# Strassen products with two-term weight sums, partial sums kept as PSUM seeds, and row sums shared with GpSimd

## The chip, the cores and the metric

The kernel runs on one core of a Trainium2 chip. The metric is the device time of one execution in microseconds (us); I give the median of the timed runs. Profiles are of one execution each, and a profile's span is a little shorter than the timed figure (276.0 against 278.06 us in the profiled execution of the kernel before). In the profile, PE is TensorE's matmuls, PEld its weight loads, DVE is VectorE, ACT is ScalarE, POOL is GpSimd, and SP issues DMAs.

## The reference

```python
x = A_x                                   # 1 x 2048 tokens x 512, bf16
for _ in range(2):
    x = x + attn(layernorm(x), wqkv, wo)  # linear attention, 32 heads of 16:
                                          #   phi(q) (phi(k)^T v) / (phi(q) . sum phi(k)),  phi(t) = t+1 or exp(t)
    x = x + relu(layernorm(x) @ w1) @ w2  # w1: 512 x 1376, w2: 1376 x 512
```

## The kernel before

The kernel builds a graph of about 1,400 operations. A fixed table, `ORDER`, lists them; each engine gets its own operations in the order of the table, runs them strictly in that order, and waits on semaphores for operations of other engines. A letter after an index chooses the engine of a flexible operation (`a` ACT, `d` DVE, and in the changed kernel `p` GpSimd). A second table, `BANKS`, gives each PSUM tile one of the eight banks. Two operations in different engines' lists have no order but what their data and their banks demand.

The second FFN product uses Strassen's seven products instead of eight, over pairs of 128-token tiles. It needs sums of hidden rows ("row sums", 128 x 1,280 elements in bf16) and sums of weight blocks, here up to four terms:

```python
T1, T2, T3, T4 = B12, w2s[:, 0, :, :], w2s[:, 1, :, :], w2s[:, 2, :, :]
tt(T3, B22, B12, ALU.add, ...)
tt(T1, B12, B11, ALU.subtract, ...)
tt(T2, B22, T1, ALU.add, ...)
tt(T4, B21, T2, ALU.subtract, ...)
...
def row_sums(t):
    def tt(n, a, b, rd):
        ap, key, own = sum_slot()
        g.add(DVE, lambda e: e.tensor_tensor(ap, a, b, ALU.subtract), ...)   # always on DVE
    tt(1, A21, A22, lo + hi)
    tt(2, A11, out[1][0], ...)
    tt(3, A21, A11, lo)
    tt(4, A12, out[2][0], ...)
```

Four times per pair, an intermediate product is scaled and added to the residual in SBUF:

```python
def part(i, bank, cols, name):
    g.add(DVE, lambda e: e.scalar_tensor_tensor(xres[:, i, cols], psv[:, bank, R], rstdf[:, i:i + 1],
                                                xres[:, i, cols], ALU.mult, ALU.add), ...)
prod("fy", raw(KH, l2), T4, ..., cb, L, True, l2)
prod("f1", raw(0, l1), B11, w, cb, R, False);           part(i1, cb, L, "r11")
prod("f5", summed(1), T1, ..., ca, R, True);            part(i2, ca, R, "r22")
prod("f6", summed(2), T2, ..., cb, R, False);           part(i1, cb, R, "r12")
...                                                     # f2, f3, f7
part(i2, cb, L, "r21")
```

Two groups of small DVE operations will play a part. One is the attention's reciprocal of the denominators, whose result TensorE waits for; the other is the variance of a chunk of 512 tokens:

```python
g.add(DVE, lambda e: e.scalar_tensor_tensor(rsp[:, s, :], rhi[:, s, :], rneg[:, 0:1], lden[:, s, :], ...))   # "rsp"
mm_group(...)                                            # denominators broadcast to 4 banks: needs rsp
for j in range(4):
    g.add(DVE, lambda e, j=j: e.tensor_tensor(unit_ap(us[j]), unit_ap(us[j]), psv[:, GB[j], :], ALU.mult))   # frees the bank
...
g.add(DVE, lambda e: e.scalar_tensor_tensor(nm2f[:, sl], nmf[:, sl], -1.0, nmf[:, sl], ...))                 # 128 x 4
g.add(DVE, lambda e: e.scalar_tensor_tensor(varf[:, sl], s2f[:, sl], INV_D, nm2f[:, sl], ...))               # 128 x 4
```

Of the kernel before, what the change touches and what calls it, by code (L numbers as in the profile page):

```python
# [14 lines left out]
C_MM512 = 216.0  # L15
# [25 lines left out]
C_POOL_TT = 1250.0  # L41
C_POOL_CP = 700.0
# [27 lines left out]
class _Graph:  # L70
# [52 lines left out]
    def add_flex(self, alts, reads=(), writes=(), name=""):  # L123
# [7 lines left out]
17 0 14 12 15 18 13 1 16 19 2 20 22 3 24 4 21 23 25 5 6 26 27 7 28 8 33 29 47 30 31 32a 34 48 40 49 35 71 50 36 41 42  # L131
51 37 43 52 73 44 38 72 53d 45 74 39a 87 56 46a 76 54 89 88 58 81 78 60 77 98 59 55 57 61 83 62 75 63 82 93 117 100
113 86 99 64 65d 66a 108 79 80 68a 90 69 103 84 67a 85 119 92 95 70 115 94 135 114 91 110 118 116 120 105 141 121 154
122 104 158 130 109 156 136 132 123 125d 131 124d 142 126d 138 128 133 157 137 155 148 139 127d 143 134 129 230 149
160 147 159 140 161 153 162 96 163 97 144 219 171 101 106 150 102 164 177 172 166d 165d 173 145 189 169 168d 167a 146
151 183 191 152 170 190 107 176 192 178 222 193 184 220 182 9 111 112 179 10 221 201 185 11 174 223 180 181 231 203
186 175 213 202 187 204 188 214 205 215 195 216 217 207 196 197 232 209 194 198 208 199 210 200 211 233 206 234 261
212 262 218 263 224 228 225 264 229 265 244 235a 237d 238a 236d 249 246 226 245 266 251 259 267 250 269 239 268 276
260 240 241 270 315 313 277 252 311 247 317 316a 314d 254 278 318d 312a 271 279 248 256 253 334 255 242 257 273 243
344 335 272 258 329 338 336 345 337a 319 330 339 320 346 331 347d 332a 301 340 321 349 341 291 342d 333 322 302 296  # L140
323 350 292 274 293 324 275 306 298 280 294 303 327 286 297 299 304 307 328 281 287 295 358 288 300 326 282 362 359d
308 283 305 364 325 348 284 355 363a 285 365a 309 388 310 343 289 227 376 356a 389 357 374 377a 290 392 390 437 375d
378 438 403 351 391d 379 352 353 372 354 439 404 380 360 373d 381 398 361a 440 382 370 399 368 441 371a 402 400 405
383 369a 366 386 401a 387 393 367a 385 406a 477 384 478 394 409 442 397 475 462 395 473 396a 452 444 407 457 408 453
447 443 456 454 474 493 455a 480 448 494 449 451 446 496 450a 463 423 464 466 445 467 417 424a 465d 476 421 418a 410
479 419 422a 411 412 481 413 414 458 420a 427 459 461 460d 497 415a 468 433 495 428a 469 425 470 434a 471 472 416 431
426d 572 429 432a 435 430a 482 436a 484 483 488 500 489 521 501 522 498 570 485 499 490 526 502 486 504 550 505 487
491 531 503 527 492 506 536 532 551a 507 547 525 509 556 508 510 571 548a 558 511 557a 512 573 513 549 530 560 523 528
537 529a 552 514 515d 516a 518d 562 561a 517d 519 559a 538 566 524d 563a 539d 553a 533 520 574 534d 567a 543 575 535
554 541 576 540 577 555a 544 542 579 578 564 580 545 546 581 565a 582 585 583 590 586 584 593 587 591 594 588 568 592  # L150
589 597 569d 595 714 618 596 715 629 620 619 716 601 630 598 621 631 622 623 602 599 635 625 717 600 643 626 624 632
633 603 666 645 604 644 606 663 605 607 667d 670 664a 627 608 609 628 665 636 671a 668 638 610 646 637 647 648 669d
634 653 649 650 611 672 612d 613a 614d 678 673a 615d 616 654 639 718 679d 655 719 640 617 651 674 641 720 676 675a 652
656 680 677a 657 682 681a 684 683a 721 685a 723 722 737 724 734 738 792 735 741 736 793 742 794 739 729 740 725 730
743 745 795 726 731 746 799 727 747 642 800 728 732 796 744 748 803 733 750 686 751 749 797 687 812 798 688 752 801
753 754 689 815 802 813 816 755 807 814 756a 819 808 758a 757d 817 759d 760 809 820 818 810 823 761 690 804 811 824
691 658 805 821 806 693 659 825 692 826 695 694 699 696 828 822 697 700 829 827 698 660 762 830 702 831 661 832 701
707 703 662 764 704 706 709 833 705 708 776 763 834a 835d 713 710 778 711 838 769 765 836a 712 768 837a 771 766 775
839 779 770 767 783 777 772 846 785 780 773 784 782 786 774 848 847 840 849 787 791 842 781 841 852 843 873 850 854
788 853 858 874 875 844 845 789 860 859 851 855 856 790 888 857 889 861 862 890 866 876 867 877 863 868 891 892 895  # L160
864 896 865 897 898 878 869a 872d 870a 871d 905 880 899 879 893 881 906 882 907 900 894 883 903 910 901 885 884 902
949 945 912 904 915 911 950d 946a 951 947 886 952a 920 948d 917 887 978 921 908 918 909 922 973 979 916 923 963 980
974 981a 968 975 964 976a 965 967 953 969 984 940 954 966d 970 977 930 971d 919 983 955 913 925 924 942 956 941 935
914 957 931 932 1012 1166 958 926 960 927 992 962 1013 1010 961 993a 937 959 1002 1011a 933 928 1014 938 1008 934
1003a 929 1015 994 1009a 1016 936 1037 943 995a 944 972 939 1032 1038 982 985 1071 1033 1017 1072 998 1019 986 1073
1034 1039 987 1006 1035d 988 1040a 1018 1004 999a 1074 1043 1021 1007a 1000 1020 1005a 1075 996 1001d 1076 997d 989
1078 1027 990a 1077 991 1022 1028 1086 1029 1031 1023 1030a 1024 1091 1025d 1026 1079 1042 1081 1041 1109 1096 1036
1087 1111 1092 1090 1107 1112 1125 1082 1114 1097 1085 1126 1093 1113 1094a 1128 1088 1098 1108 1048 1100 1115 1051
1099a 1127 1083 1095 1089d 1116 1102 1110 1084a 1130 1118 1049a 1131 1101 1052a 1117 1119 1129 1080 1135 1050 1121
1120 1132 1136 1122 1133 1167 1137 1123 1150 1134 1138 1155 1124 1145 1151 1139 1140 1152 1156 1153a 1053 1146 1157  # L170
1147 1149 1055 1158d 1141 1148a 1063 1142 1144 1143d 1161 1061 1168 1159 1154 1180 1169 1160 1065 1056a 1044 1162
1064a 1163 1045 1103 1059 1164 1104 1054a 1165 1105 1046 1181a 1067 1062a 1106 1057 1066a 1060a 1176 1047 1069 1068a
1177 1058a 1182 1178 1070a 1184 1183a 1179 1197 1185a 1170 1267 1198a 1199 1171a 1265 1191 1200a 1201 1172 1266 1192a
1214 1202a 1186 1193 1195 1203 1268 1196a 1173 1194 1215a 1187 1208 1174a 1189 1204 1209a 1218 1175 1190a 1231 1188
1205 1210 1219a 1216 1223 1232d 1225 1224a 1217d 1212 1235 1213a 1226d 1220 1236a 1227 1206 1233 1207a 1221 1242 1250
1211 1243a 1222 1248 1234d 1251a 1269 1244 1237 1228 1254 1249a 1245 1238 1270 1229 1239 1271 1252 1230a 1246 1253a
1274 1247a 1255 1259 1272 1260a 1275 1240 1256 1273 1279 1241a 1261 1263 1280 1283 1264a 1262 1257 1281 1284 1258a
1282 1276 1298 1302 1285 1303 1299 1277 1304 1286 1278 1288 1287 1307 1300 1290 1289 1305 1301 1293 1308 1316 1294
1331 1317 1291 1306 1318 1309 1332 1295 1321 1292 1312 1322 1310 1296 1319 1311 1297 1335 1333 1336 1334 1326 1349
1337 1320 1338 1327 1350 1339 1323 1351 1313 1328 1324 1329 1340 1325 1314 1360 1341 1315 1354 1345 1330 1355 1352  # L180
1346 1356 1353 1361 1347 1342 1348 1362 1343 1357 1367 1358 1344 1363 1359 1366 1364 1368 1365
"""
BANKS = ("0145324562706310713073037377010377101337703107013101701070073333700656655033141302741603645322705013"
         "6431645710222077055722557250202702550722705057572520720507270507252572220575725077545320570423052463"
         "720156456671340275034631527643015276410235")


def _replay(ops, tile_ops, vbank, partial, seeded, order_s, banks_s):
# [15 lines left out]
    for pos, w in enumerate(table):  # L204
        o = ops[int(w.rstrip("ad"))]
        if o.alts:
            eng = {"a": ACT, "d": DVE}[w[-1]]
            o.eng, o.emit, o.dur = [x for x in o.alts if x[0] == eng][0]
# [24 lines left out]
    return order, max(o.t_done for o in ops)  # L233


def build_kernel(nc, A_x, A_wqkv, A_wo, B_w1, B_w2, out, n_layers_pairs=2, Q_LATE=3, O_PE_CHUNKS=3, PHI_PATH=3,
                 KV_LAG=2, INTERLEAVE=True, WARM=10, SPLIT_CHUNKS=1, TAIL_SPLIT=True,
                 PHI_K=3, PHI_QE=3, PHI_QL=3, ZH_FIRST=True, P2_TIGHT=False,
                 FIRST_PE_CHUNKS=1, TGK=2, TGF=2, FT_PE=0, WP_GB=True, WO_LAG=1, DEN_PRE=1, LATE_A=1, ZP=(0, 3), WK_ACT=False, ACT_STATS=(), REM_TOK=True, RSTD_ACT=(0, 1, 2, 3), FILL=(0,), NFILL=2, HEAD_DEP=0, ST_ACT=True, H_STR=[0, 1, 2, 3, 4], NSUM=6):
# [977 lines left out]
```

## Time and profile before

The median of three runs is 278.93 us (278.34 to 279.35); with a fourth run, as in the result below, it is 278.75. The lines below are from the profile page of the kernel before: the span, the busy times by engine with their share of the span, the busy tenths of PE and POOL in 40 slices of the span, the granted TensorE clock in tenths, and the chain of waits followed back from the last instruction.

```profile
span 276.0 us, 4814 instructions
...
PE 270.5 (98%) x1794; PEld 153.1 (55%) x1794; DVE 237.2 (86%) x600; ACT 178.0 (65%) x372; POOL 34.4 (12%) x43
...
PE   7999999999999999999999999999999999999995
...
POOL 3111000001002021032003464000000005000000
PEclk9999999999999999999999999999999999999999
...
PE 94%; DVE 2%; DMA 2%; ACT 0%; issue 0%; SPq 0%; DVEq 0%
```

TensorE is busy 98% of the time and every slice but the first and the last is at 9 tenths or more. The chain of waits stays on TensorE for 94% of the span. TensorE's own list of waits (line, what released it, us in total, times, longest) says the same:

```profile
PE ps L407 <- DVE wrm L400: 1.2, 1, 1.2
PE ps L486 <- DVE xn L967: 0.4, 1, 0.4
PE ps L523 <- DMA Tb<-xn: 0.3, 1, 0.3
PE ps L523 <- ACT Tb L493: 0.3, 1, 0.3
```

That is 2.2 us in the whole program. DVE is busy 86%, but nothing waits long for it.

One interaction is visible. GpSimd has few large operations before, the adds of 512 columns at L580. This is the timeline of the kernel before around one of them (start in us, duration, engine, line, operation):

```profile
...
158.31 0.43 DVE L509 TENSOR_TENSOR big<-big,emscr 128x512 bf16<-128x512 bf16 x1
...
158.82 1.16 POOL L580 TENSOR_TENSOR lden<-lden,big 128x512 f32<-128x512 f32 x1 [1.09 <-DVE big L509]
...
158.97 1.28 DVE L509 TENSOR_TENSOR big<-big,emscr 128x512 bf16<-128x512 bf16 x1
```

The DVE add takes 0.43 us when it runs alone and 1.28 us when it starts just after a GpSimd add: it ends 0.27 us after that one. I call the excess over an instruction's clear duration "held" time. Summed over the trace before, DVE is held for 8.5 us, all of it in the attention stages and none of it where TensorE waits.

### The profile page before, as it was taken

To read this page: it belongs to the slowest core of one execution; us is meant where nothing else is said; L and a number is where in the kernel's file an instruction comes from. 1 tells how busy PE (TensorE), PEld (TensorE's weight loads), DVE (VectorE), ACT (ScalarE), POOL (GpSimd) and SP (SyncE) were. 2 spreads that over 40 slices of the span, in tenths; PEclk is the share of its full clock that TensorE was granted. 3 is DMA by queue.
4 is the path that set the end of the run, shared out by engine and by line. 5 is a ranking of instruction groups with operands and counts; after the bars stand their busy time and mean duration, and the time that the engine had idled before them with its cause. 6 is when DMAs were issued, how large, how long until landed. Compare 5 with 4: busy or idle time off the path is not lost.

```text
span 276.0 us, 4814 instructions
## 1 busy us (share of the span) xinstructions
PE 270.5 (98%) x1794; PEld 153.1 (55%) x1794; DVE 237.2 (86%) x600; ACT 178.0 (65%) x372; POOL 34.4 (12%) x43
## 2 busy tenths in 40 slices
PE   7999999999999999999999999999999999999995
PEld 2444544344465657655877444443447745568883
DVE  5999669999996795998689777799999997978996
ACT  4998838996776195486254987689947279762000
POOL 3111000001002021032003464000000005000000
PEclk9999999999999999999999999999999999999999
DMA  6946950120142018003005030003022450300014
GB/s 207 381 99 112 292 161 0 37 41 20 38 78 57 0 21 153 2 20 76 2 0 59 20 76 0 2 1 76 4 57 40 95 148 8 38 0 2 0 78 152
DMA packets 41974, 18.32 MB, mean 66 GB/s; under 512 B 36352, under 2 KB 40544, under 8 KB 41952
## 3 DMA queue, kind: packets, MB, share of 16 engines
q1 hardware_dynamic: 41808, 17.96, 27.7%
q8 instruction: 14, 0.23, 0.3%
q10 hardware_dynamic: 144, 0.07, 0.1%
q14 instruction: 8, 0.07, 0.1%
HBM read 7.01 MB, written 2.10 MB: 33 GB/s over the span
## 4 chain that ended last, share of the span: by engine, by line
PE 94%; DVE 2%; DMA 2%; ACT 0%; issue 0%; SPq 0%; DVEq 0%
PE ps L523 93%; DMA xin<-in_A_x_dram 1%; DMA Tb<-xn 1%; DVE xres L536 1%; DVE xn L563 1%; PE ps L486 0%; DVE xn L543 0%; DVE bst L430 0%; ACT Tb L493 0%; DVE nmf L539 0%; SPq L371 0%; DVEq L1155 0%; DVE xn L967 0%; DVE emscr L507 0%; DVE big L509 0%
## 5 line engine op out<-in xcount | busy, mean ns | idle before, releaser
L523 PE MATMUL ps<-Tb,w 128*128 128x512 bf16 x260 | 61.1, 379 | 0.3 <-DMA Tb<-xn 0.3
L530 ACT ACTIVATE sqscr<-xres 128x512 bf16<-128x512 f32 x48 | 30.0, 626 | 24.7 <-DVE xres L567 19.1
L505 ACT ACTIVATE escr<-ps 128x512 bf16<-128x512 f32 x64 | 38.3, 615 | 7.5 <-PE ps L523 6.4
L523 PEld LDWEIGHTS ps<-Tb,w 128*128 128x128 bf16 x260 | 24.9, 98 | 28.4 <-DMA Tb<-xn 0.6
L503 ACT ACTIVATE big<-ps 128x512 bf16<-128x512 f32 x64 | 37.7, 615 | 3.8 <-PE ps L523 3.6
L893 DVE SCALAR_TENSOR_TENSOR xres<-ps,rstdf,xres 128x256 f32<-128x256 f32 x64 | 30.0, 480 | 9.0 <-PE ps L523 8.4
L724 ACT ACTIVATE big<-ps 128x512 bf16<-128x512 f32 x50 | 28.5, 598 | 9.4 <-PE ps L523 9.4
L523 PE MATMUL ps<-w,big 128*128 128x256 bf16 (+1 forms) x224 | 33.9, 273 | 0.0
L523 PE MATMUL ps<-Tb,wqkv 128*128 128x512 bf16 x138 | 33.2, 379 | 0.0
L509 DVE TENSOR_TENSOR big<-big,emscr 128x512 bf16<-128x512 bf16 x64 | 29.8, 479 | 2.1 <-ACT big L503 0.8
L523 PE MATMUL ps<-wqkv,Tb 128*128 128x512 bf16 x128 | 30.8, 379 | 0.3 <-ACT Tb L493 0.3
L523 PE MATMUL ps<-big,xn 128*128 128x512 bf16 x128 | 30.9, 379 | 0.0
L523 PE MATMUL ps<-Wp,big 128*128 128x512 bf16 x128 | 30.1, 379 | 0.0
L556 POOL TENSOR_TENSOR rstdf<-varf,nhalf 128x4 f32<-128x4 f32 x8 | 9.1, 1146 | 122.5 <-DVE varf L554 122.5
L523 PEld LDWEIGHTS ps<-w,big 128*128 128x128 bf16 (+1 forms) x224 | 21.8, 98 | 4.6 <-DVE xres L893 0.3
L523 PE MATMUL ps<-w,xin 128*128 128x256 bf16 x160 | 22.6, 272 | 0.0
L507 DVE TENSOR_SCALAR emscr<-escr 128x512 bf16<-128x512 bf16 x64 | 19.4, 317 | 3.1 <-ACT escr L505 2.9
L523 PEld LDWEIGHTS ps<-Tb,wqkv 128*128 128x128 bf16 x138 | 13.2, 98 | 15.5 <-issue 0.5
L523 PE MATMUL ps<-w2s,xin 128*128 128x256 bf16 x160 | 21.7, 273 | 0.0
L681 DVE TENSOR_TENSOR big<-big,ps 128x512 bf16<-128x512 bf16 x32 | 20.7, 681 | 0.4 <-PE ps L523 0.4
L523 PEld LDWEIGHTS ps<-wqkv,Tb 128*128 128x128 bf16 x128 | 12.1, 98 | 15.1 <-ACT Tb L493 1.0
L523 PEld LDWEIGHTS ps<-Wp,big 128*128 128x128 bf16 x128 | 12.1, 98 | 14.3 <-issue 0.5
(126 smaller groups left out, 379.6 us busy)
## 6 DMA issues: line engine op xcount, KB each, us to landing
wqkv<-in_A_wqkv_dram SPq DMA_DIRECT2D x3, 512.0 KB, 7.4
xin<-in_A_x_dram SPq DMA_DIRECT2D x3, 512.0 KB, 8.2
out_dram<-xn SPq DMA_DIRECT2D x3, 512.0 KB, 2.6
w<-in_B_w_dram SPq DMA_DIRECT2D x1, 1376.0 KB, 6.5
w<-in_B_w_dram SPq DMA_DIRECT2D x1, 1280.0 KB, 9.7
wo<-in_A_wo_dram SPq DMA_DIRECT2D x1, 512.0 KB, 10.2
Tb<-xn SPq DMA_TRANSPOSE x30, 3.2
xin<-in_A_x_dram SPq DMA_DIRECT2D x1, 384.0 KB, 3.1
```

The costliest lines, as they stand in the source:

```text
L503: g.add(ACT, lambda e: e.activation(dst_ap, psv[:, b, :], ACTF.Identity, bias=1.0 + 1e-6, scale=1.0), [("ps", b)], [dst_key], C_ACT_PSUM, ...
L505: g.add(ACT, lambda e: e.activation(escr[:, s, :], psv[:, b, :], ACTF.Exp), [("ps", b)], [("escr", s)], C_ACT_EXP, name=name + "_exp")
L507: g.add(DVE, lambda e: e.tensor_scalar(emscr[:, s, :], escr[:, s, :], 1.0, 1e-6, ALU.min, ALU.add), [("escr", s)], [("emscr", s)], C_DVE_B ...
L509: g.add(DVE, lambda e: e.tensor_tensor(dst_ap, dst_ap, emscr[:, s, :], ALU.max), [dst_key, ("emscr", s)], [dst_key], 340.0, name=name + "_ ...
L523: last = e.matmul(o, l, r, start=st, stop=sp, skip_group_check=skip)
L530: g.add(ACT, lambda e: e.activation(sqscr[:, q, :], xres[:, i, :], ACTF.Square, accum_out=dst[:, i:i + 1]), [("xres", i)], [("sqscr", q), ...
L536: g.add(DVE, lambda e: e.scalar_tensor_tensor(xres[:, i, :], psv[:, b, :], 0.0, src, ALU.add, ALU.add, accum_out=s1f[:, i:i + 1]), [("ps", ...
L556: g.add(POOL, lambda e: e.tensor_tensor(rstdf[:, sl], varf[:, sl], nhalf[:, 0:4], ALU.pow), [("varf", t), ("nhalf",)], [("rstdf", t)], C_P ...
L563: g.add(DVE, lambda e: e.scalar_tensor_tensor(xn[:, i, :], psv[:, b, :], rstdf[:, i:i + 1], xres[:, i, :], ALU.mult, ALU.add), rd, [("xn", ...
L681: g.add(DVE, lambda e, j=j: e.tensor_tensor(unit_ap(us[j]), unit_ap(us[j]), psv[:, GB[j], :], ALU.mult), [("big", us[j]), ("ps", GB[j])], ...
L724: g.add_flex([(ACT, lambda e, M=M, b=b, u=u: e.activation(unit_ap(u, M), psv[0:M, b, :], ACTF.Relu), C_ACT_PSUM), (DVE, lambda e, M=M, b=b ...
L893: g.add(DVE, lambda e: e.scalar_tensor_tensor(xres[:, i, cols], psv[:, bank, R], rstdf[:, i:i + 1], xres[:, i, cols], ALU.mult, ALU.add), ...
```

## The change

The intent is to relieve DVE. Both FFN Strassen products are put in forms whose weight operands are differences of two blocks. In the second FFN product, two of the four partial sums per pair are no longer added to the residual by DVE; they are copied from one PSUM bank into another, where the next products accumulate on top of them ("seeds"; 23 of the 32 copies on ACT, 9 on DVE). The remainder products of 96 rows are merged to 512 columns. The hidden product of the last FFN is done per chunk of 512 tokens instead of over a pair of chunks. Sums become flexible between DVE and GpSimd, and the table puts 17 of them on GpSimd: 11 row sums, one sum of w1 blocks (both 128 x 1,280) and five sums of activations (128 x 512). The order and bank tables are new throughout.

```diff
-            tt(T3, B22, B12, ALU.add, ...)
-            tt(T1, B12, B11, ALU.subtract, ...)
-            tt(T2, B22, T1, ALU.add, ...)
-            tt(T4, B21, T2, ALU.subtract, ...)
+            tt(E1, B11, B22, ...)
+            tt(E2, B12, B22, ...)
+            tt(E3, B21, B22, ...)
+            tt(B12, B12, B11, ...)          # in place
+            tt(B21, B21, B11, ...)          # in place
 ...
 def row_sums
-                g.add(DVE, lambda e: e.tensor_tensor(ap, a, b, ALU.subtract), ...)
+                g.add_flex([(x, lambda e: e.tensor_tensor(ap, a, b, op), c)
+                            for x, c in ((DVE, C_DVE_SUM), (POOL, C_POOL_SUM))], ...)
 ...
 def b_out_pair
-            prod("fy", ...); prod("f1", ...); part(i1, cb, L, "r11")
-            prod("f5", ...); part(i2, ca, R, "r22")
-            prod("f6", ...); part(i1, cb, R, "r12")
-            ...      ; part(i2, cb, L, "r21")
+            def seed(cols, name):
+                g.add_flex([(ACT, lambda e: e.activation(psv[:, c1, cols], psv[:, c2, L], ACTF.Identity), 290.0),
+                            (DVE, lambda e: e.tensor_copy(psv[:, c1, cols], psv[:, c2, L]), 330.0)], ...)
+            prod("f1", summed(1), B22, ...);  seed(R, "r12")
+            prod("f2", summed(4), B11, ...);  part(i2, c2, R, "q21", L)
+            prod("f6", summed(2), E1, ...);   part(i2, c2, L, "q22", R)
+            prod("f7", raw(KH, l2), E3, ...); seed(L, "r11")
+            prod("f5", raw(0, l2), B12, ...); rem(c2, l2, slice(0, D), i2)
+            prod("f3", ...); prod("f4", ...); rem(c1, l1, slice(0, D), i1)
 ...     (the hidden product: per chunk in two 256-token halves, sums on DVE or GpSimd; cut)
-ORDER = """ ... 1,369 entries
+ORDER = """ ... 1,403 entries, 17 of them with p
```

## The prediction

> **What bounds the kernel now.** TensorE, almost alone. The page gives PE 98% busy; the chain of waits is 93% matmuls at one line, and PE's own list of waits holds only 2.2 us, nearly all of it in the first 6 us. Busy time can hide slow issue, so I took the distances between matmul starts from the trace: a 512-column matmul follows the last after 216 ns (median), a 256-column one after 109 ns, a 96-column one after 43 ns. The program streams 642,136 columns. Counted at those distances, that accounts for all but about 4 us between 8.5 us (start of steady work) and 272.7 us (last matmul). About 2.4 us of these 4 sit around the tiled denominator matmuls (some 100 ns at each change, both ways), which stay. About 1.5 us are real waits: 0.45 us at 190.8 us (a transpose DMA), 0.2 us at 271.5 us, the rest near 0.1 us each. DVE is 86% busy, ACT 65%, GpSimd 12%; none of them holds TensorE up for long.
>
> **What the change does.**
> - TensorE: columns unchanged, 642,136 (seven products instead of eight in both kernels and in the same places). The hidden-layer Strassen moves from a pair of 512-token chunks to two 256-token halves of one chunk: 70 matmuls of 512 columns become 140 of 256, +0.2 to +0.4 us at 216 and 109 to 110.6 ns. Most remainder matmuls merge from 256 to 512 columns: about -0.15 us. Net about +0.2 us.
> - DVE: 32 of 64 partial-sum updates go (480 ns each, -15.4 us). 32 seed copies come, 23 on ACT, 9 on DVE (estimate 0.4 us each from 700 ns for 512 columns: +3.5 us). 11 of 32 row sums go to GpSimd (819 ns each, -9.0 us). Strassen epilogues, weight sums and relus together about +1 us. DVE loses about 20 us.
> - ACT: +23 half-size copies, about +9 us, with 98 us idle today.
> - GpSimd: 12 sums of 1,280 columns, 2.9 us each (estimate from 1.156 us for its 512-column add), and five of 512 columns: about +41 us, from 34 to 75.
>
> **A new cost.** The Trainium skill, "SBUF — State Buffer", section "SBUF: two separate sides", says that GpSimd and certain DVE instructions take a shared port pair as an exclusive lock. The trace agrees: the bf16 tensor-tensor of 420 ns takes up to 1,405 ns when a GpSimd add runs, the 287 ns tensor-scalar up to 1,243, while instructions reading PSUM keep their 480 and 680 ns. So each GpSimd sum can hold DVE up to 2.9 us; I expect 8 to 18 us of such holding, returning most of DVE's relief, and some late evacuations that stall TensorE, 0.3 to 1.5 us in all.
>
> **How much is on the critical path.** Almost nothing: DVE's relief is off it. Gains: about 0.3 us at the end (before, two 0.74 us residuals queue ahead of the last half output; now one overlaps the last product), up to 0.7 us from the stalls. Losses: 0.2 us of smaller matmuls, 0.3 to 1.5 us of new stalls.
>
> **Prediction.** 278.6 us, range 277.2 to 280.8. Faster by over 2%: 0.01; within 2%: 0.95; slower by over 2%: 0.04.
>
> **What would show it.** PE busy stays near 270 us, its columns and distances unchanged; DVE falls from 237 to 215-230 us; ACT rises to about 187, GpSimd to about 75; GpSimd sums near 2.9 us; DVE two-input sums over 1 us beside them; span 274.5 to 278.
>
> **What would make it wrong.** GpSimd sums much longer than 2.9 us, or DVE held just where a bank is awaited (then slower: the last chunk has few independent products); or smaller matmuls costing more than 110 ns each; or the granted clock falling below 1.00.

## The result

The changed kernel took 286.68 us (286.03 to 287.17, four runs), beside 278.75 us for the kernel before in the same rounds. The ratio is 1.0281 (95% interval 1.0253 to 1.031). A ratio here is the mean time of one kernel's fast runs over the mean of the other's fast runs of the same rounds, so it is not quite the ratio of the quoted medians. Where I turn a difference of ratios into microseconds below, I multiply it by 278.8 us.

The page of the changed kernel, the same lines:

```profile
span 284.3 us, 4892 instructions
...
PE 271.4 (95%) x1814; PEld 156.4 (55%) x1833; DVE 235.6 (83%) x572; ACT 184.6 (65%) x393; POOL 73.7 (26%) x60
...
PE   8998999999969999999999998999999898999995
...
POOL 3111000001462201233011757000009965147000
PEclk9999999999999999999999999999999999999999
...
PE 68%; DVE 18%; DMA 9%; ACT 3%; issue 1%; SPq 0%
```

The work of TensorE is the same: 271.4 us busy instead of 270.5. The span grew by 8.3 us, so about 7.4 us of it is new idle time of TensorE. POOL went from 34.4 to 73.7 us. DVE, which was to be relieved, is busy 235.6 instead of 237.2 us. In this execution the clock is 9 tenths or more in every slice, so its 8.3 us are no change of clock. It is the fastest of the four (286.03 us, mean granted clock 0.999); the other three, 286.65 to 287.17 us, have a mean of 0.994. An estimate: 0.6% of 285 us is 1.7 us, what a stretch of 3.4 us at half clock takes away; such stretches do stand in the traces of other runs below. The mean of the four lies 0.6 us above the profiled execution. The chain of waits leaves TensorE for a third of its length. TensorE's list of waits:

```profile
PE ps L528 <- DVE big L689: 2.2, 1, 2.2
PE ps L528 <- DMA Tb<-xn: 1.4, 2, 0.8
PE ps L412 <- DVE wrm L405: 1.2, 1, 1.2
PE ps L528 <- DVE big L514: 1.2, 1, 1.2
PE ps L528 <- DVE xn L568: 0.8, 1, 0.8
```

The wait for wrm at the start stands in both kernels. The first, fourth and fifth of these lines are new waits for DVE. No wait of TensorE for GpSimd is listed, no part of the chain lies on GpSimd, and DVE's own waits for GpSimd are one of 0.4 us, which stands in the run with all sums on DVE too: in this trace it is not the results of the sums that come late. Here is the timeline of the changed kernel around the first, 2.2 us long:

```profile
...
74.67 5.61 POOL L879 TENSOR_TENSOR xin<-big 128x1280 bf16<-128x1280 bf16 x2 [4.30 <-ACT big L732]
74.72 3.10 DVE L683 SCALAR_TENSOR_TENSOR rsp<-rhi,rneg,lden 128x512 bf16<-128x512 bf16 x1
...
77.75 2.47 DVE L689 TENSOR_TENSOR big<-big,ps 128x512 bf16<-128x512 bf16 x4
...
80.27 0.39 PE L528 MATMUL ps<-rsp,esel 32*128 32x512 bf16 x4 [2.17 <-DVE big L689]
```

A GpSimd row sum starts at 74.67 and a second follows it at 77.24 (the 5.61 us of the first line join the two; each is 2.6 to 3.1 us long). The DVE instruction rsp starts 0.05 us after the first and takes 3.10 us instead of its clear 0.75. The four multiplications that free the PSUM banks come after it, and TensorE idles 2.17 us until 80.27. The other two waits for DVE have the same picture. This is the one at 241.5 us:

```profile
...
238.18 2.60 POOL L879 TENSOR_TENSOR emscr<-big,escr 128x1280 bf16<-128x1280 bf16 x1 [2.20 <-PE ps L528]
238.25 2.55 DVE L557 SCALAR_TENSOR_TENSOR varf<-s2f,nm2f 128x4 f32<-128x4 f32 x1
...
240.72 1.40 DVE L568 SCALAR_TENSOR_TENSOR xn<-ps,rstdf,xres 128x512 bf16<-128x512 f32 x2
...
241.52 0.61 PE L528 MATMUL ps<-xn,w 128*128 128x256 bf16 x4 [0.80 <-DVE xn L568]
```

A variance of 128 x 4 elements, 0.16 us when clear, took 2.55 us beside a sum that started 0.07 us before it, and what stood behind it on DVE came too late for TensorE. In all, DVE is held for 19.2 us in this trace, against 8.5 before.

The line "DMA Tb<-xn" is a wait of another kind. Of its 1.4 us, 0.6 stand at 25.5 us. The other 0.8 are these: the transposes of chunk 2 for the last FFN were issued at 221.29 us, the second landed 4.6 us later, and TensorE stood at the first product of chunk 2's hidden layer until then.

So there were two theories of the 8 us. One says that the GpSimd sums hold DVE and that this is all. Its rival says that the new order is to blame: TensorE's list asks for products before their inputs can be there, whatever GpSimd does. A third possibility is that the new forms themselves cost time.

### The profile page after: what moved, and what is told of

The parts are those of the page before. It is cut to its first block, busy times and chain, and to the rows that moved or that the text cites. A ratio compares the mean times of both kernels' runs of the same rounds, so it can differ in the third digit from the quotient of the medians.

```text
span 284.3 us, 4892 instructions
## 1 busy us (share of the span) xinstructions
PE 271.4 (95%) x1814; PEld 156.4 (55%) x1833; DVE 235.6 (83%) x572; ACT 184.6 (65%) x393; POOL 73.7 (26%) x60
## 4 chain that ended last, share of the span: by engine, by line
PE 68%; DVE 18%; DMA 9%; ACT 3%; issue 1%; SPq 0%
PE ps L528 67%; DMA Tb<-xn 4%; DMA w<-in_B_w_dram 3%; DVE xres L541 2%; DVE bst L435 2%; DVE emscr L512 2%; DVE rsp L683 2%; DVE big L514 1%; DVE xn L568 1%; DMA xin<-in_A_x_dram 1%; DVE varf L557 1%; DVE big L689 1%; DVE w2s L397 1%; ACT escr L510 1%; DVE GT L618 1%
## 5 line engine op out<-in xcount | busy, mean ns | idle before, releaser
L528 PE MATMUL ps<-Tb,w 128*128 128x512 bf16 x240 | 56.6, 379 | 0.0
L528 PEld LDWEIGHTS ps<-Tb,w 128*128 128x128 bf16 x240 | 22.7, 98 | 25.4 <-DVE big L733 0.5
L528 PE MATMUL ps<-Tb,wqkv 128*128 128x512 bf16 x128 | 30.0, 379 | 0.2 <-issue 0.2
L512 DVE TENSOR_SCALAR emscr<-escr 128x512 bf16<-128x512 bf16 x64 | 22.3, 364 | 8.0 <-ACT escr L510 7.7
L514 DVE TENSOR_TENSOR big<-big,emscr 128x512 bf16<-128x512 bf16 x64 | 27.0, 439 | 1.6 <-ACT big L508 0.6
L917 DVE SCALAR_TENSOR_TENSOR xres<-ps,rstdf,xres 128x256 f32<-128x256 f32 x32 | 15.2, 482 | 10.8 <-PE ps L528 10.6
L528 PE MATMUL ps<-w2s,big 128*128 128x256 bf16 x160 | 22.2, 272 | 0.1
L528 PE MATMUL ps<-w,big 128*128 128x256 bf16 (+2 forms) x113 | 21.9, 302 | 0.0
L528 PEld LDWEIGHTS ps<-big,xn 128*128 128x128 bf16 x128 | 11.9, 98 | 14.5 <-DVE big L514 1.9
L528 PE MATMUL ps<-w,xin 128*128 128x256 bf16 x140 | 19.4, 273 | 0.0
```

Source lines behind the costliest of these rows:

```text
L512: g.add(DVE, lambda e: e.tensor_scalar(emscr[:, s, :], escr[:, s, :], 1.0, 1e-6, ALU.min, ALU.add), [("escr", s)], [("emscr", s)], C_DVE_B ...
L514: g.add(DVE, lambda e: e.tensor_tensor(dst_ap, dst_ap, emscr[:, s, :], ALU.max), [dst_key, ("emscr", s)], [dst_key], 340.0, name=name + "_ ...
L528: last = e.matmul(o, l, r, start=st, stop=sp, skip_group_check=skip)
```

## The experiments

The quoted expectations call the theory of the GpSimd sums A, refer to earlier runs by the first part of their labels (e1, e4, ...), and say what each rival expects. All kernels gave correct results.

### All sums back on DVE

```diff
-ORDER: 474p 475p 476p 854p 1121p ... 1330p     (17 entries)
+ORDER: 474d 475d 476d 854d 1121d ... 1330d
```

> All 17 tensor sums that the change gave to GpSimd go back to DVE, at the same places of the order; nothing else. Theory A (GpSimd sums hold DVE instructions, and three of those holds reach TensorE: 2.34 us at 77.7 us, 1.30 us at 175.5 us, 0.97 us and perhaps 0.49 us at 240 us): 281.0 to 282.5 us instead of 286.7, DVE held time falls from 19 to about 9 us (the z sums stay), DVE busy about 238 us. Rival B (DVE was relieved and needs it; the loss is in the new order or the new forms): 286 to 290 us, since DVE gets 12 x 0.82 + 5 x 0.41 = 12 us more work.

It took 284.37 us (283.23 to 284.73), ratio 1.0202 (1.0162 to 1.0242). Held time fell to 8.1 us, the level of before, yet only 2.2 us of the 7.8 came back. The wait beside rsp fell from 2.2 to 0.6 us and the one beside the variances is gone. What remains is led by the wait for the transposes (timeline of this run):

```profile
...
218.47 2.62 SPq L474 DMA_TRANSPOSE Tb<-xn  x2
...
223.13 0.62 PE L528 MATMUL ps<-Tb,xin 128*128 128x256 bf16 x4 [2.09 <-DMA Tb<-xn]
```

The wait is now longer than in the change (2.09 us in this line against 0.83) and it is followed by a stretch of 3.41 us in which the clock record shows half speed, so it costs more than itself. The one execution of four with a granted clock of 0.999 took 283.23 us; the other three, at 0.993 and 0.994, took 284.19 to 284.73. Theory A alone fell here: the lock is part of the loss, and the order has a loss of its own.

### Only three sums back on DVE

In the trace of the change, three GpSimd sums stood beside the three longest holds.

```diff
-ORDER: 474p 854p 1240p
+ORDER: 474d 854d 1240d
```

> Only the three GpSimd sums beside which DVE was held over 2.3 us go to DVE (the first row sum of chunk 0 in the first FFN, one hidden-weight sum, the fourth row sum of chunk 1 in the last FFN). Theory A: nearly the whole of what all 17 give back, 281 to 283 us; the other 9 large sums hold DVE where TensorE does not wait for it. Theory A' (every sum costs alike): a quarter of it, 285 us. Rival B: no gain.

It took 285.97 us (284.07 to 287.37), ratio 1.0262 (1.0211 to 1.0313), which is not clear of the change. The four executions spread with the clock: 284.07 us at a granted clock of 1.000, 287.37 at 0.987. The trace is of the last, the slowest. The holds at the second and third place vanished with their waits. At the first place they did not. The next GpSimd sum moved up and held the same instruction:

```profile
...
74.30 2.61 POOL L879 TENSOR_TENSOR xin<-big 128x1280 bf16<-128x1280 bf16 x1 [4.31 <-ACT big L732]
74.35 3.11 DVE L683 SCALAR_TENSOR_TENSOR rsp<-rhi,rneg,lden 128x512 bf16<-128x512 bf16 x1
```

TensorE then waited 2.9 us there, and a stretch of 6.83 us at half clock began near the end of the wait. A sum that is removed is replaced by the one behind it in GpSimd's list, so single sums can't be blamed by name from this run.

### The same three sums, but later

Here the three sums stay on GpSimd, and each waits for the DVE instruction that it had held.

```diff
+        for late, held in ((474, 442), (854, 1089), (1240, 1179)):
+            g.ops[late].sdeps.append(g.ops[held])        # and 1240p moves behind 1179 in ORDER
```

> All 17 sums stay on GpSimd, but the same three wait each for the DVE instruction that it had held. Theory A (where they fall, not that GpSimd does them): 282 to 284 us, the waits of TensorE at 77.7 and 175.5 us gone. If GpSimd work as such slowed DVE or came too late: no gain, or slower.

It took 283.89 us (283.63 to 284.63), ratio 1.0196, so 2.4 us of the 7.8 came back without taking any work from GpSimd. The rsp instruction was clear again, but the delayed sums met the next small DVE operations:

```profile
...
75.42 5.17 POOL L879 TENSOR_TENSOR xin<-big 128x1280 bf16<-128x1280 bf16 x2 [5.17 <-DVE rsp L683]
...
78.33 2.28 DVE L555 SCALAR_TENSOR_TENSOR nm2f<-nmf 128x4 f32<-128x4 f32 x1
...
80.55 2.60 POOL L879 TENSOR_TENSOR xin<-xin,big 128x1280 bf16<-128x1280 bf16 x1
...
80.64 2.52 DVE L557 SCALAR_TENSOR_TENSOR varf<-s2f,nm2f 128x4 f32<-128x4 f32 x1
```

Both are 0.15 us when clear. TensorE waited 2.0 us for what came after them. Here when the sums run decided what they cost.

### The first 400 entries of the order of before

```diff
-ORDER[0:~400] of the change
+ORDER[0:400] of the kernel before (operations renumbered), then the rest of the change
```

> The first 400 entries of the order (the first attention layer and the start of the first hidden layer, to about 72 us) are taken from the kernel before, with its engines and banks; the rest is unchanged, GpSimd sums included. Theory C (a second part of the loss is the regenerated order in the attention layer that the change does not touch: waits of 0.77 us at 24.5, 0.26 us at 48.3, 0.2 to 0.9 us before 10 us): 284.7 to 285.7 us. If the head only looks slow because loads landed later in that one execution: 286.3 to 287 us.

It took 291.79 us (289.9 to 292.32), ratio 1.0463. This is a miss of construction. The splice put the hidden products of chunk 1 right behind the attention, a GpSimd sum held the normalization in front of its transposes, and TensorE waited 6.6 us for them from 72 us on. It does not isolate what the head of the order costs, and I draw nothing from it but one more example of a held operation ahead of a DMA.

### The kernel before with the same row sums on GpSimd

This takes the suspected cause alone into the kernel before: its forms, its order, and its 11 row sums of the same names moved to GpSimd.

```diff
-                g.add(DVE, lambda e: e.tensor_tensor(ap, a, b, ALU.subtract), ...)
+                g.add(POOL if (t, n) in share else DVE, lambda e: e.tensor_tensor(ap, a, b, ALU.subtract), ...)
```

> The kernel before, its forms and its order untouched; only the 11 row sums that the change gives to GpSimd (by chunk and number) run there. Each takes 2.6 us instead of 0.82. Theory A (the shared port: DVE instructions with two SBUF inputs or of the small statistics wait while a GpSimd sum runs): DVE held time rises from 8.5 to over 15 us and the kernel gets 1.5 to 4 us slower, 280 to 282.5 us, though DVE loses 9 us of work. Rival D (sharing is free where the order has room): within 0.7 us of before, 277.8 to 279 us.

It took 283.97 us (283.95 to 284.44), ratio 1.019 (1.0168 to 1.0212): 5.3 us from moving the sums alone, above the range that I had expected. DVE's busy time hardly moved, 234.7 us instead of 237.2, although 11 sums of 0.82 us had left it; it is held for 14.1 us. New lines stand in TensorE's list:

```profile
PE ps L523 <- DVE big L820: 3.0, 2, 2.1
...
PE ps L523 <- DVE big L681: 1.0, 1, 1.0
```

This shows the direction without the new forms or the new order. But the largest of these waits is not one of holding. The timeline of this run shows a DVE sum that waits until two GpSimd sums have ended:

```profile
...
233.33 5.17 POOL L858 TENSOR_TENSOR xin<-big 128x1280 bf16<-128x1280 bf16 x2
...
238.54 0.82 DVE L858 TENSOR_TENSOR xin<-big,xin 128x1280 bf16<-128x1280 bf16 x1 [5.44 <-POOL xin L858]
...
240.02 0.85 PE L523 MATMUL ps<-w,Tb 128*128 128x96 bf16 x16 [2.14 <-DVE big L820]
```

DVE stood idle for 5.44 us, and TensorE waited 2.1 us for what came behind that sum in DVE's list. So in this kernel the lateness of the results is a second way in which the sums cost time. In the traces of the change and of the other runs with these 17 sums DVE does not wait for a sum on GpSimd. The 5.3 us also contradict the small share that the first run gave to the sums. The next runs deal with that.

### Chunk 2's hidden product later

Starting from the run with all sums on DVE, five operations move back in the table: the first product of chunk 2's hidden layer with its copy, and chunk 2's remainder. One PSUM tile also gets another bank.

```diff
-ORDER: ... 1120 1124d 1206 1084a 1127 1207a 1237d ... 1128 1182 1167 1156 1183d 1184 1161 ...
+ORDER: ... 1120 1124d 1084a 1127 1237d ... 1170 1171 1182 1206 1183d 1207a 1184 1191a ...
```

> On top of the run with all sums on DVE: the first hidden-layer Strassen product of chunk 2 of the last FFN and the remainder products of that chunk stand 7 groups later in TensorE's order, behind the attention products of chunk 3 (about 4.5 us). Theory E (the new order asks for the transposed activations of chunk 2 before they can have landed: 2.25 us of waiting at 220.7 us and a 3.4 us stretch at half clock after it): 281 to 282.5 us against 284.4. If the wait only moves to another instruction: 284 us.

It took 281.64 us (281.59 to 282.44), ratio 1.0101 (1.0077 to 1.0126). The difference of the two ratios to the kernel before, which allow for runs on different occasions, makes it 2.8 us faster than with all sums on DVE alone. The 2.1 us wait for chunk 2's transposes is gone, and so is the stretch at half clock (a wait of 0.6 us for other transposes, at 25 us, stands in both). This part of the order theory is confirmed.

### Both: chunk 2 later, and the sums on GpSimd

```diff
-ORDER: 474d 475d 476d 854d 1121d ... 1330d     (of the run above)
+ORDER: 474p 475p 476p 854p 1121p ... 1330p
```

> The fourth corner of a square of four: the change itself (286.7 us: sums on GpSimd, chunk 2's hidden product early), e1 (284.4: sums on VectorE, early), e8 (281.6: sums on VectorE, late), and this one (the change with chunk 2's hidden product late, its 17 sums still on GpSimd). If the two causes add, the wait for the transposes of chunk 2 (1 to 2 us and the stretch at half clock) goes and the GpSimd cost of 2.3 us stays: 283.4 to 284.6 us, ratio 1.016 to 1.021. If the GpSimd sums cost what they cost in e4 and e11 (5 to 6 us) once the other wait is gone, that is, the two waits hid each other in the change: 286 to 287.5 us, ratio 1.026 to 1.032.

It took 285.61 us (285.08 to 286.75), ratio 1.0251 (1.0224 to 1.0279), between the two expectations. The four ratios to the kernel before form a square:

| | sums on GpSimd | sums on DVE | cost of the GpSimd sums |
|---|---|---|---|
| chunk 2's product early | 1.0281 (the change) | 1.0202 | 2.2 us |
| chunk 2's product late | 1.0251 | 1.0101 | 4.2 us |
| gain of moving it | 0.8 us | 2.8 us | |

An estimate of the noise, from the intervals of the ratios taken as independent: 2.2 and 2.8 us are known to about 1.4 us, 4.2 us to 1.0, and 0.8 us, known to 1.1, is not clear of zero.

The two causes do not seem to add. With one of them in place, the other costs about 2 us less than alone (known to about 1.7 us). The traces show a reason: with the sums on GpSimd TensorE comes to chunk 2's product later and waits 0.8 us for the transposes instead of 2.1. The clock has a share in it too. In the executions with a granted clock of 0.998 or more (one of the change, one with the sums on DVE and chunk 2 early, all four with chunk 2 late on DVE, two of this run), each taken less the mean of the kernel before in its rounds, the sums cost 2.6 and 3.3 us and the move gains 0.9 and 1.6 us, so that only 0.7 us of overlap is left. This explains a part of the contradiction: the first run saw a small cost of the sums partly because the late transposes were still there.

### The new forms with a searched order

To see whether the forms cost anything, I searched order, banks and the engines of the flexible operations of the changed graph anew, against a model that uses durations measured in these traces. The first 300 entries come from the kernel before, and no sum is on GpSimd.

```diff
-ORDER, BANKS of the change
+ORDER, BANKS searched; sums all with d
```

> The new forms with all their instructions, no sum on GpSimd, but another order, engine choice for the flexible copies and bank table: the first 300 entries are those of before, the rest was searched with the durations measured here. Theory F (the forms cost nothing, the order of the change costs): 277 to 279.5 us, level with before, TensorE's waits under 2 us. Rival G (the new forms themselves hold TensorE: seeds, chained partial sums in one bank, 256-column products): 281 us or more, with waits at the output products.

It took 277.69 us (277.46 to 277.96), ratio 0.9961 (0.994 to 0.9982). The page shows:

```profile
span 276.0 us, 4889 instructions
...
PE 270.1 (98%) x1816; PEld 157.6 (57%) x1833; DVE 230.5 (84%) x591; ACT 182.9 (66%) x391; POOL 34.8 (13%) x43
...
PE 93%; DVE 3%; DMA 2%; ACT 1%; issue 1%
```

TensorE is busy 98% as in the kernel before, and its list of waits holds 1.2 us at the start and three short waits of 0.4 us and less. In this order the forms cost nothing that can be seen, and this is the fastest kernel, by 1.1 us of 278.8. The third theory fell.

### A control: the kernel before, searched in the same way

> Control for e6: the kernel before (old forms, all its row sums on VectorE) with its order searched by the same procedure and the same measured durations, no other edit. If the search and not the new forms gave e6 its 1.1 us: 277.2 to 278.0 us, ratio 0.994 to 0.998, level with e6. If the new forms gave it (VectorE free of two updates a pair): 278.3 to 279.2 us, ratio 0.998 to 1.003, as before. Over 280 would say that the searched order is worse for the old forms and the control says nothing.

```diff
-ORDER, BANKS of before
+ORDER, BANKS searched
```

It took 281.62 us (280.65 to 282.36), ratio 1.0084. The searched order lost 1.7 us in two waits at 174.4 and 175.5 us, where GpSimd's adds of the attention held DVE one after the other (the first of the two is for a GpSimd result), and a stretch of 3.41 us at half clock followed. By the expectation a time over 280 says nothing about the forms. So it stays open whether the 1.1 us of the run above come from the forms or from its particular order. What the control does show is that the search by itself does not give a faster kernel.

### The searched order with the 17 sums on GpSimd

```diff
-ORDER: 474d 476d 475d 1121d ... 1330d     (of the searched order)
+ORDER: 474p 476p 475p 1121p ... 1330p
```

> The order of e6 (277.69 us, no 1,280-column sum on GpSimd) with the same 17 sums on GpSimd that the change puts there; no other edit. Theory A (GpSimd's sums hold VectorE statistics and evacuations and this costs TensorE waits wherever they stand): 280 to 283.5 us, ratio to before 1.005 to 1.018, held VectorE time 14 to 22 us instead of 7.8, and waits of TensorE of over 0.5 us beside GpSimd sums. Rival (the sharing is harmless once the order has room; it hurt only because the change's order was late elsewhere): 277.5 to 278.7 us, held time up but no new waits.

It took 283.72 us (283.44 to 284.87), ratio 1.0173 (1.0141 to 1.0206): 5.9 us more than the same order with the sums on DVE (the difference of the two ratios is 0.0212). Held time rose from 7.8 to 21.0 us. Three waits come back:

```profile
PE ps L528 <- DVE xn L788: 1.7, 1, 1.7
PE ps L528 <- DVE big L733: 1.7, 1, 1.7
PE ps L528 <- DVE rsp L683: 1.3, 1, 1.3
```

Theory A is confirmed for an order that otherwise keeps TensorE fed: the sums cost 5.9 us here (known to about 1.1 us; the ratio lies in the expected range, the time 0.2 us above it). The 5.3 us in the kernel before contain waits for late results as well.

### Dummy sums on GpSimd

A sum takes GpSimd 2.6 us and DVE 0.82 us. The cost could come from that lateness and not from the holding. So here all real sums stay on DVE, and GpSimd adds 17 sums of weights of the same sizes into a buffer that is idle. They wait for the same producers as the real ones, and nothing reads them. (A few more waits keep the borrowed buffer safe.)

```diff
+        for real in (474, 476, 475, 1121, ..., 1330):
+            o = g.add(POOL, lambda e, n=n: e.tensor_tensor(gt2[:, :, 0:n], w1[:, 0:2, 0:n], w1[:, 2:4, 0:n], ALU.subtract), ...)
+            o.sdeps.extend(d for d in g.ops[real].sdeps ...)
```

> The order of e6 (277.69 us) with all sums on VectorE as there, and GpSimd adds 17 dummy sums of the same sizes, released by the same producers as the real ones and placed as in e11 (283.72 us); nothing reads their results (they go to a buffer that is idle then). If holding VectorE is what costs (lock): most of the 6 us of e11 comes back, 280.5 to 285 us, ratio 1.007 to 1.023, held VectorE time 15 to 25 us. If it is the lateness of results, since a sum takes GpSimd 2.6 us and VectorE 0.8: 277.5 to 279 us, ratio 0.995 to 1.002, though held time rises all the same.

It took 291.07 us (290.1 to 292.32), ratio 1.043 (1.0409 to 1.0451), 13.1 us over the searched order and above the range of both expectations. Held time was 23.9 us. The timeline first shows what the run was made for. At the same place as in the previous run, a sum on GpSimd holds rsp, and TensorE waits the same 1.3 us for it; but here nothing reads the sum:

```profile
...
74.13 5.62 POOL L1140 TENSOR_TENSOR GT<-w 128x1280 bf16<-128x1280 bf16 x2 [49.55 <-ACT sqscr L535]
...
74.57 2.71 DVE L683 SCALAR_TENSOR_TENSOR rsp<-rhi,rneg,lden 128x512 bf16<-128x512 bf16 x1
...
77.34 0.40 PE L528 MATMUL ps<-rsp,esel 32*128 32x512 bf16 x4 [1.32 <-DVE rsp L683]
```

It also shows where the excess comes from, at least in part: a dummy is released at the same moment as the real sum, starts first, and holds it.

```profile
...
209.18 5.31 POOL L1140 TENSOR_TENSOR GT<-w 128x1280 bf16<-128x1280 bf16 x2 [36.39 <-ACT big L732]
...
211.94 3.24 DVE L879 TENSOR_TENSOR escr<-big 128x1280 bf16<-128x1280 bf16 x1
```

The second of the two joined dummies starts at 211.87. A DVE sum of 0.82 us took 3.24 beside it. By my sum over the trace 10 of the 23.9 us held fall on real sums, and two stretches of 3.41 us at half clock add to the time (the profiled execution is the slowest, 292.32 us). So holding alone is enough to make TensorE wait, without any result of GpSimd being late. The size doesn't carry over to the change, because here the sums burden both engines.

### A search that was allowed 22 sums on GpSimd

> As the last, but the search could give sums to GpSimd and knew that a GpSimd sum holds those DVE instructions: 22 sums are there, more than the 17 of the change. If where the sums fall is what costs: within 0.7 us of the last run, 276.8 to 279.5 us. If GpSimd sums always cost: 2 us or more above it.

```diff
-ORDER, BANKS searched; sums all with d
+ORDER, BANKS searched; 22 sums with p, with a model of the holding
```

It took 302.44 us (302.09 to 304.07), ratio 1.086. DVE was held for 38.4 us. The model had assumed that GpSimd runs a sum at its place in the table. On the chip it starts as soon as the inputs are there, and four sums of weights ran back to back:

```profile
...
180.59 10.72 POOL L761 TENSOR_TENSOR xin<-w 128x1280 bf16<-128x1280 bf16 x4
...
183.30 8.29 DVE L514 TENSOR_TENSOR big<-big,emscr 128x512 bf16<-128x512 bf16 x3
...
191.65 0.40 PE L528 MATMUL ps<-ones,big 128*128 128x1 bf16 x9 [10.08 <-DVE big L514]
```

Between two successive sums DVE gets one instruction through: three adds of 0.4 us took 8.29 us, and TensorE waited 10.1 us; a stretch of 10.24 us at half clock began in that wait. The expectation that placing alone decides failed by over 20 us, though with a model that placed the sums wrongly.

## Why the prediction was wrong

The prediction was 278.6 us with a range of 277.2 to 280.8, and a chance of 0.04 for slower by over 2%. The kernel took 286.68 us. I go through its steps.

- "TensorE, almost alone" and the unchanged columns were right. TensorE's busy time moved by 0.9 us. The median distances are again 216, 109 and 43 ns. (The trace of the changed kernel lacks 19 matmul records of 512 columns; with these its 632,408 recorded columns are the 642,136 of before.) The smaller matmuls of the hidden layer were no cause: the searched order has the same ones and spans 276.0 us, as before.
- "DVE loses about 20 us" failed in its result: 235.6 us, outside the stated 215 to 230. The removed work was as priced (32 updates of 480 ns and 11 sums of 819 ns, less 9 copies of 428 ns, some 20.5 us). Holding returned 10.7 us of it, within the stated 8 to 18. Most of the rest are four more relus and two more copies on DVE, 4.1 us by the sums of their lines; some 4 us I did not trace.
- ACT at 184.6 us and GpSimd at 73.7 us were near the stated 187 and 75. A GpSimd sum of 1,280 columns took 2.60 to 2.65 us instead of the estimated 2.9 (one, beside rsp, took 3.05).
- The holding of DVE was foreseen with the right cause. The Trainium skill, page "SBUF — State Buffer", section "SBUF: two separate sides", describes an exclusive lock that the first comer keeps for its whole instruction. These traces agree: the rsp instruction ended at 77.82, after the sum that had started 0.05 us before it at 74.67, 3.10 us instead of 0.75.
- The step that failed is "some late evacuations that stall TensorE, 0.3 to 1.5 us in all", and with it "Almost nothing" for the critical path. The new idle time of TensorE measured about 7.4 us. Nor were evacuations what was held: in the change, DVE instructions that read PSUM took the same beside a GpSimd sum as elsewhere (at most 0.48 us for the partial sums, 0.69 and 0.75 us for the residuals). They came late because they stood behind held ones. The runs isolate two things behind the idle time; a third part stays open.

The first is a wrong conversion from held time to waits. The prediction argued from shares of busy time ("DVE is 86% busy ...; none of them holds TensorE up for long"). What counts is the place in the chain. Of the six holds by large sums in the trace of the change, five caught rsp, nm2f or varf, on which a whole chunk waits: its reciprocal, its normalization, its transposes, its next matmuls. (In the kernel before with the row sums on GpSimd, the holds caught other instructions, of 128 x 512.) How much passes on depends on the place: in the three longest holds, 2.4 us each on rsp, on the 128 x 512 operation at L512 and on varf, TensorE waited 2.2, 1.2 and 0.8 us, and a hold of 2.0 us on nm2f shows no such wait. Four measurements of moving the sums alone give 2.2 and 4.2 us (in the order of the change), 5.3 us (in the kernel before, late results included) and 5.9 us (in the searched order). The prediction did name "DVE held just where a bank is awaited" as what would make it wrong, and gave it too little weight.

The second is something that the prediction never priced: the order table was regenerated, and it asks for chunk 2's hidden product before its transposes can have landed. This costs 2.8 us when the sums are on DVE and 0.8 us, not clear of zero, when they are on GpSimd.

How the 7.8 us divide cannot be given as one sum, since the causes overlap. Taken away in one sequence, they are: the GpSimd sums 2.2 us, chunk 2's product 2.8 us, the rest of the order (with the engines of the flexible copies) 3.9 us, and the kernel then stands 1.1 us below before. The 3.9 us, the largest part, were not taken apart further. In the profiled executions TensorE is idle for 10.5 us with chunk 2 later and 5.9 us in the searched order. Of the 4.5 us between them 1.5 fall before 12 us, mostly in one wait of 1.3 us that the other runs with this order don't show, and the rest are many waits of 0.6 us and less. So that part is shown to cost and not shown why. The possible gains that the prediction listed, up to 1 us, are of the size of what the searched order showed, but the control doesn't tell whether they come from the forms.

## What to carry to other kernels

In a kernel whose TensorE is 98% busy, moving work from DVE to GpSimd is not free capacity: here a GpSimd sum of 2.6 us held the DVE instruction behind it by up to 2.4 us, so ask which short DVE operation stands next to it and who waits for that one. A GpSimd operation starts when its inputs are ready, not at its place in a schedule table, so tie it to a moment where DVE reads PSUM or has slack, or leave it on DVE. Ask also who reads its result, which comes after 2.6 us and not 0.82. When a diff carries a regenerated order, price the order too, by asking for each product when its last input lands.

## What the Trainium skill lacked or had wrong

- Page "SBUF — State Buffer", section "SBUF: two separate sides": the lock is as described, and the page's rule for two SBUF inputs covers even statistics of 128 x 4 elements, which grew from 0.16 to 2.55 us. What the page lacks is a picture of GpSimd operations back to back: four sums of 10.72 us in all let DVE through one instruction at a time, three in 8.29 us.
- Page "GPSIMD Engine Reference", section "4.1 Engine selection": it gives roughly twice the time of VectorE for a two-input elementwise operation. For 1,280 bf16 columns these runs show 2.60 us against 0.82 us, a factor of 3.2, and it does not say there that the operation also stops VectorE.
- Page "TensorE: Matmul & The Clock Gate", "Part 1: The HAM clock gate (the "warmup" mystery)": it puts the slow clock after an idle window of about 3.4 us. These runs show half clock for 3.41 us after a wait of 2.1 us (all sums on DVE), for 3.41 us after two waits of 0.9 and 0.8 us within 2 us (the searched control), and for 6.83 us with one of 2.9 us (three sums on DVE), but none after one of 2.2 us (the profiled execution of the change; its other three have a mean clock of 0.994). So a wait shorter than that window can be enough, and nearly equal waits need not cost the same. The page calls the window free-running, which may be why; no run here tests it.
- No page read says how to price a GpSimd operation by what it holds: here moving 11 to 17 sums cost 2.2 to 5.9 us, depending on the order around them.
